# Seven waits for stores behind the block's closing barrier, and no GpSimd drain in that barrier

## Chip, core and metric

The kernel runs on one core of a Trainium2 chip. The metric is the device time of one execution in microseconds (us). Three runs of the kernel before the change took 148.33, 148.35 and 148.73 us; the median is 148.35.

## What is computed

The input x has 2048 rows of 640 numbers (bf16). Each row is normalised, and three things are added: x itself, a spectral filter of the normalised rows, and a two-layer network of them.

```python
def _A_ref(x, w_r, w_i):
    X = rfft2(x.astype(float32), axes=(-2, -1))
    X = X * (w_r + 1j * w_i)
    return irfft2(X, s=(S, D), axes=(-2, -1)).astype(bfloat16)

def _B_ref(x, w1, b1, w2, b2):
    h = gelu(x @ w1 + b1)          # 640 -> 1536
    return h @ w2 + b2             # 1536 -> 640

xn = layernorm(A_x)
out = A_x + _A_ref(xn, A_w_r, A_w_i) + _B_ref(xn, B_w1, B_b1, B_w2, B_b2)
```

## The kernel before

The 2048 rows are worked on as 16 chunks c of 128 rows. Early stages load x and the weights (SyncE's queue, L375), normalise, transpose, run the first layer of the network (results in `gT`) and the forward and inverse transforms as matmuls against tables. TensorE works on all of this nearly without a gap. The last stage, for each chunk c, adds up in PSUM the second layer and the last step of the inverse transform (L383); VectorE adds the bias row and writes the finished chunk into SBUF (L787); one DMA brings it to the output in HBM.

There are 18 such final stores. Chunks 0 to 13 go by GpSimd's queue (L794), each as an accumulating DMA onto a copy of x that was put into the output earlier. Chunks 14 and 15 go by SyncE's queue (L791) as plain DMAs: chunk 14 in one store, chunk 15 in three (320, 160 and 160 columns), since its sum is made in three pieces. So GpSimd issues 14 stores, and SyncE issues 4. Each store has a semaphore of its own, which reaches 16 when the data has landed.

What each engine does, and in which order, is a list written out by hand (`ORDER`, set up by `arrange`). `sync` works out which waits an operation needs, and `emit` puts the lists into the program: it opens a block (`nc.Block()`), in which every engine gets its own body. In a body each operation is preceded by its waits (L233). SyncE's body ends with a loop over the list `last`, that is the 18 stores, and waits for each (L244).

When the block closes, every engine leaves its body by a branch and meets the others at a barrier. The block is closed by the `with ExitStack()` statement, so the profile shows the instructions of that barrier under L319: a DRAIN on each engine, which on four of them counts up a semaphore; GpSimd waits for the four (EVENT_SEMAPHORE) and releases them with a second instruction; each of the four waits for that release. The program opens with a barrier of the same make, which the profile shows under L813. The kernel has no instruction of its own behind the closing barrier.

Of the kernel before, what the change touches and what calls it, by code (L numbers as in the profile page):

```python
# [121 lines left out]
class Sched:  # L122
# [7 lines left out]
    def op(self, engs, prio, emit, reads=(), writes=(), after=(), gate=(), segs=None, dma=None, late=0.0, group=None, hard=()):  # L130
        o = Op()
        o.name = writes[0].name if writes else ""
        o.engs, o.prio, o.emit, o.segs, o.dma, o.late, o.group = engs, prio, emit, segs, dma, late, group
        o.reads, o.writes, o.gate, o.hard = list(reads), list(writes), list(gate), list(hard)
        o.seq = len(self.ops)
        o.eng, o.inc, o.count, o.sem = None, False, None, None
        o.deps = [w for b in o.reads for w in b.writers] + list(after)
        for b in o.reads:
            b.readers.append(o)
        for b in o.writes:  # L140
            b.writers.append(o)
        self.ops.append(o)
        return o
# [69 lines left out]
    def emit(self, es, last):  # L213
        nc = self.nc
        sems = {e: nc.alloc_semaphore(f"s_{e}") for e in self.engines if e != "sp"}
        shared = {g: nc.alloc_semaphore(f"g_{g}") for g in self.groups}
        for e in self.engines:
            n = 0
            for o in self.order[e]:
                if o.group:  # L220
                    o.sem, o.count = shared[o.group], 16 * len(self.groups[o.group])
                elif o.dma:
                    o.sem, o.count = nc.alloc_semaphore(f"d_{o.seq}"), 16
                elif o.inc:
                    n += 1
                    o.sem, o.count = sems[e], n
        block = es.enter_context(nc.Block())

        def run(name):
            def go(e):  # L230
                for o in self.order[name]:
                    for d in o.waits:
                        e.wait_ge(d.sem, d.count)  # L233
                    ins = o.emit(e, name)
                    if o.dma:
                        ins.then_inc(o.sem, 16)
                    elif o.inc:
                        ins.then_inc(o.sem, 1)
                if name == "sp":
                    seen = set()  # L240
                    for o in last:
                        if (o.group or o) not in seen:
                            seen.add(o.group or o)
                            e.wait_ge(o.sem, o.count)  # L244
            return go
        block.sync(run("sp"))
        block.gpsimd(run("pool"))
        block.vector(run("dve"))
        block.scalar(run("act"))
        block.tensor(run("pe"))  # L250
# [46 lines left out]
def bass_parallel_sum__spectral_gfnet__dense_activation_gelu__prompt_kernel(  # L297
# [21 lines left out]
    with ExitStack() as es:  # L319
# [478 lines left out]
        K.sync()  # L798
        K.emit(es, last)


# [1 line left out]
_INS = ['A_x', 'A_w_r', 'A_w_i', 'B_x', 'B_w1', 'B_b1', 'B_w2', 'B_b2']  # L803
# [24 lines left out]
```

## Time and profile before

| what | value |
|---|---|
| median of three runs | 148.35 us |
| the profiled execution, its own time | 148.24 us |
| its span, first to last instruction | 146.4 us |
| granted TensorE clock over the span | 1.000 |
| TensorE matmuls busy | 142.3 us |
| VectorE, ScalarE, GpSimd busy | 110.6, 76.2, 21.4 us |

Times in the profile count from the first instruction of the span. PE is TensorE, DVE VectorE, ACT ScalarE, POOL GpSimd and SP SyncE; a name with a q (SPq, POOLq) is an engine's sequencer, which handles waits, branches and the issue of DMAs. In the rows of one source line, the three numbers behind the count are the shortest, median and longest duration in ns, and "first and last start" are in us. "DMA to landing" counts from the start of the issue to the landing of the data. The execution's own time is longer than its span: something at the start or the end of an execution lies outside the recorded instructions.

### The profile page before, as it was taken

How to read it: one execution, taken by the hardware profiler on the slowest of the kernel's cores; microseconds unless marked ns; L12 is line 12 of the kernel's file. 1: busy time of each engine (PE TensorE's matmuls, PEld its weight loads, DVE VectorE, ACT ScalarE, POOL GpSimd, SP SyncE). 2: the span in 40 equal slices, each digit the busy share in tenths (PEclk: the TensorE clock that was granted, in tenths of full speed). 3: DMA queues.
4: the chain of work that ended last, by engine and by line, in shares of the span. 5: the costliest groups of instructions: out<-in, count | busy, mean ns of one | idle time of the engine just before them, and what ended most of it. 6: DMA issues, size and time to landing. Idle time of an engine off the chain costs nothing.

```text
span 146.4 us, 3965 instructions
## 1 busy us (share of the span) xinstructions
PE 142.3 (97%) x1685; PEld 89.3 (61%) x1685; DVE 110.6 (76%) x237; ACT 76.2 (52%) x125; POOL 21.4 (15%) x35
## 2 busy tenths in 40 slices
PE   7899999999999999999999999999999999999992
PEld 7799995655566545445545455555576665655571
DVE  1898999999994459659959999471059995996571
ACT  3517995158786697887678554143445471300000
POOL 1102031211010041000000000000000125526240
PEclk9999999999999999999999999999999999999999
DMA  4999999669999989908300932515300307976685
GB/s 118 322 396 399 348 385 217 161 135 95 183 176 185 206 230 330 358 23 115 67 4 10 118 63 42 117 24 111 69 4 0 45 5 89 118 81 83 81 100 124
DMA packets 27923, 21.00 MB, mean 143 GB/s; under 512 B 20226, under 2 KB 25090, under 8 KB 27779
## 3 DMA queue, kind: packets, MB, share of 16 engines
q1 hardware_dynamic: 24528, 15.03, 43.5%
q0 software_dynamic: 2592, 4.92, 18.3%
q10 hardware_dynamic: 786, 0.82, 2.4%
q8 instruction: 13, 0.21, 0.6%
q14 instruction: 4, 0.02, 0.0%
HBM read 13.54 MB, written 5.24 MB: 128 GB/s over the span
## 4 chain that ended last, share of the span: by engine, by line
PE 94%; DVE 2%; DMA 2%; issue 0%
PE ps L383 93%; DMA X<-in_A_x_dram 2%; DVE stats L483 1%; PE ps L531 1%; DVE T L513 0%; DVE mv L485 0%; DVE W L787 0%; DVE xnT L395 0%; DVE rstd L491 0%; DVE ve L493 0%
## 5 line engine op out<-in xcount | busy, mean ns | idle before, releaser
L383 PE MATMUL ps<-xnT,W 128*128 128x512 bf16 (+2 forms) x336 | 57.7, 320 | 0.1
L383 PE MATMUL ps<-W,gT 128*128 128x512 bf16 (+3 forms) x396 | 57.6, 296 | 0.0
L383 PEld LDWEIGHTS ps<-W,gT 128*128 128x128 bf16 x396 | 30.1, 98 | 22.8 <-issue 1.5
L383 PEld LDWEIGHTS ps<-xnT,W 128*128 128x128 bf16 x336 | 31.6, 114 | 17.3 <-issue 2.2
L614 ACT ACTIVATE gT<-ps,b1col 128x512 bf16<-128x512 f32 (+1 forms) x48 | 28.9, 637 | 6.8 <-PE ps L383 6.6
L794 POOL DMA_DIRECT2D out_dram<-W x14 | 12.2, 902 | 74.0 <-DVE W L787 74.0
L483 DVE BATCH_NORM_STATS2 stats<-X 128x6 f32<-128x320 bf16 x32 | 13.9, 479 | 2.2 <-DMA X<-in_A_x_dram 2.2
L394 ACT ACTIVATE Wf<-ps 128x960 bf16<-128x960 f32 (+1 forms) x9 | 7.6, 880 | 12.0 <-PE ps L383 7.0
L394 ACT ACTIVATE XV<-ps 128x1280 bf16<-128x1280 f32 (+2 forms) x8 | 8.8, 1104 | 7.7 <-PE ps L383 7.7
L681 DVE TENSOR_TENSOR T<-Y,Wf 128x1288 bf16<-128x1288 bf16 x16 | 12.5, 824 | 0.1
L494 POOL TENSOR_TENSOR rstd<-ve,mhalf 128x2 f32<-128x2 f32 (+1 forms) x8 | 6.2, 770 | 33.1 <-DVE ve L493 33.1
L394 ACT ACTIVATE Xb<-ps 128x960 bf16<-128x960 f32 (+1 forms) x7 | 8.0, 1165 | 3.8 <-PE ps L383 3.8
L395 DVE CAST Y<-ps 128x644 bf16<-128x644 f32 x8 | 6.6, 828 | 4.0 <-PE ps L383 3.9
L547 DVE TENSOR_TENSOR T<-T 128x128 bf16<-128x128 bf16 (+1 forms) x32 | 8.5, 320 | 0.1
L394 ACT ACTIVATE T<-ps 128x512 bf16<-128x512 f32 (+1 forms) x14 | 5.4, 442 | 6.0 <-PE ps L383 6.0
L395 DVE CAST Xb<-ps 128x960 bf16<-128x960 f32 (+1 forms) x5 | 5.5, 1110 | 3.8 <-PE ps L383 3.8
L787 DVE TENSOR_TENSOR W<-ps,X 128x640 bf16<-128x640 f32 x7 | 5.7, 822 | 2.4 <-PE ps L383 2.4
L543 DVE TENSOR_TENSOR T<-T 128x640 bf16<-128x640 bf16 x16 | 7.4, 488 | 0.2
L513 DVE TENSOR_SCALAR T<-X,mv,rstd 128x640 bf16<-128x640 bf16 x16 | 6.7, 432 | 1.1 <-POOL rstd L494 1.1
L394 ACT ACTIVATE Y<-ps 128x644 bf16<-128x644 f32 x8 | 5.7, 708 | 3.4 <-PE ps L383 3.4
L383 PE MATMUL ps<-etab,XV 32*128 32x160 bf16 (+1 forms) x128 | 7.2, 232 | 0.0
L383 PE MATMUL ps<-Wf,htab 128*128 128x512 bf16 (+3 forms) x33 | 7.1, 295 | 0.0
(55 smaller groups left out, 127.4 us busy)
## 6 DMA issues: line engine op xcount, KB each, us to landing
out_dram<-in_A_x_dram POOLq DMA_DIRECT2D x4, 640.0 KB, 7.3
X<-in_A_x_dram SPq DMA_DIRECT2D x7, 320.0 KB, 8.8
out_dram<-W POOLq DMA_DIRECT2D x14, 160.0 KB, 3.5
W<-in_B_w_dram SPq DMA_DIRECT2D x5, 384.0 KB, 5.4
W<-in_B_w_dram SPq DMA_DIRECT2D x3, 640.0 KB, 12.4
Wf<-in_A_w_i_dram SPq DMA_DIRECT2D x7, 160.5 KB, 4.0
Wf<-in_A_w_r_dram SPq DMA_DIRECT2D x5, 160.5 KB, 3.5
gtab<-c_G SPq DMA_DIRECT2D x1, 512.0 KB, 7.4
```

The lines of the kernel that those rows point to most:

```text
L383: ins = e.matmul(o_, lhsT=lw, rhs=rh, start=st, stop=sp_, skip_group_check=True)
L394: return e.activation(dst(), src(), ACT.Copy, scale=scale)
L395: return e.tensor_copy(dst(), src())
L483: st_ops.append(K.op([("dve", 0.393)], pr, lambda e, _, c=c, h=h: e.bn_stats(stats[:, c, 6 * h:6 * h + 6], view(X, c * D + H2 * h, [[1, H2 ...
L494: K.op([("pool", 0.75)], 400 + pr, lambda e, _, a=a, b=b: e.tensor_tensor(out=rstd[:, a:b], in0=ve[:, a:b], in1=mhalf[:, a:b], op=ALU.pow) ...
L513: o = K.op([("dve", 0.356)], pr, lambda e, _, c=c, n=n, xnv=xnv: e.tensor_scalar(out=xnv(n, 0, [[1, D]]), in0=view(X, c * D, [[1, D]]), sc ...
L543: K.op([("dve", 0.39)], pr, lambda e, _, k=k, op=op, xnv=xnv, x1v=x1v: e.tensor_tensor(out=x1v(H2 * k, [[D, 2], [1, H2]]), in0=xnv(0, 0, [ ...
L547: ring_ops.append(K.op([("dve", 0.333 if w == 128 else 0.136)], pr, lambda e, _, op=op, x1v=x1v, xfv=xfv, o_=o_, o0=o0, o1=o1, w=w: e.tens ...
L614: K.op([("act", act_us(128 * nt, 1) + 0.02)], pr + PRIO["gelu"], lambda e, _, c0=c0, nt=nt, fc=fc, hps=hps: e.activation(gT[:, fc, 128 * c ...
L681: filt_ops.append(K.op([("dve", 0.738)], pr, lambda e, _, k=k, Y=Y, TB=TB, pair=pair: e.tensor_tensor(out=view(TT, TB.slot * 8 * KP + k * ...
L787: K.op([("dve", dve_us(w))], 95, lambda e, _, os_=os_, fps=fps, o0=o0, w=w, xo=xo, base=base: e.tensor_tensor(out=view(W1, OST + os_.slot ...
L794: last.append(K.op([("pool", 0.9)], 450, lambda e, _, c=c, os_=os_: e.dma_start(ov[:, c, :], view(W1, OST + os_.slot * D, [[1, D]]), accum ...
```

## The change

SyncE's body no longer ends with waits. The list `rest` holds seven stores: the last three of GpSimd's and all four of SyncE's. SyncE waits for these seven after the block has closed, so behind the barrier. For the other eleven stores of GpSimd, SyncE waits inside its body, ahead of its second store. The block is opened with `no_gpsimd_drain=True`, so that it closes without GpSimd's DRAIN.

```diff
-        block = es.enter_context(nc.Block())
+        stores = {e: [o for o in self.order[e] if o in last] for e in ("pool", "sp")}
+        self.rest = stores["pool"][-3:] + stores["sp"]
+        block = es.enter_context(nc.Block(no_gpsimd_drain=True))
 
         def run(name):
             def go(e):
                 for o in self.order[name]:
+                    if o is stores["sp"][1]:
+                        for d in stores["pool"][:-3]:
+                            e.wait_ge(d.sem, d.count)
                     for d in o.waits:
                         e.wait_ge(d.sem, d.count)
                     ins = o.emit(e, name)
...
                         ins.then_inc(o.sem, 1)
-                if name == "sp":
-                    seen = set()
-                    for o in last:
-                        if (o.group or o) not in seen:
-                            seen.add(o.group or o)
-                            e.wait_ge(o.sem, o.count)
             return go
...
         K.sync()
         K.emit(es, last)
 
+    for o in K.rest:
+        nc.sync.wait_ge(o.sem, o.count)
```

## The prediction

> **What bounds the kernel now.** I read the page first, then the chain that ended last, then the last 2.5 us instruction by instruction, because the change touches nothing earlier.
>
> ```profile
> span 146.4 us, 3965 instructions
> ...
> PE 142.3 (97%) x1685; PEld 89.3 (61%) x1685; DVE 110.6 (76%) x237; ACT 76.2 (52%) x125; POOL 21.4 (15%) x35
> ...
> PE 94%; DVE 2%; DMA 2%; issue 0%
> ```
>
> TensorE sets the time up to its last matmul. What follows is the tail, and the chain of waits in order of time shows where it begins:
>
> ```profile
> 139.80 3.85 PE ps L383 x41
> 143.65 0.03 issue
> 143.68 0.33 DVE W L787
> ```
>
> The last VectorE add ends at 143.68 + 0.33 = 144.01. The span ends at 146.44, so 2.43 us hang on no engine's arithmetic. The table by stretches divides them (columns: the stretch, its length, busy time of PE, PEld, DVE, ACT and POOL, clock, DMA share, GB/s):
>
> ```profile
> 144.00:144.50 0.50, 0.00 (x0) 0.00 (x0) 0.00 (x1) 0.00 (x0) 0.00 (x0) 1.00 0.93 253
> 144.50:145.60 1.10, 0.00 (x0) 0.00 (x0) 0.00 (x0) 0.00 (x0) 0.00 (x0) 1.00 0.22 51
> 145.60:146.44 0.84, 0.00 (x0) 0.00 (x0) 0.00 (x0) 0.00 (x0) 0.00 (x0) 1.00 0.00 0
> ```
>
> In the last 0.84 us no engine computes and no DMA moves a byte. To see what stands there, I took the rows of the last SyncE store, of the waits at L244 (all nine, the first four, the last) and of the closing barrier at L319:
>
> ```profile
> L791 SPq DMA_DIRECT2D out_dram<-W x1: 333/333/333, 144.0 to 144.0; - x1
> ...
> DMA to landing us min/median/max: 1.5/1.5/1.5
> ```
>
> ```profile
> L244 SPq EVENT_SEMAPHORE  x9: 17/28/28, 144.4 to 145.6; - x9
> ...
> L244 SPq EVENT_SEMAPHORE  x4: 17/28/28, 144.4 to 144.6; - x4
> ...
> L244 SPq EVENT_SEMAPHORE  x1: 27/27/27, 145.6 to 145.6; - x1
> ```
>
> ```profile
> L319 POOLq EVENT_SEMAPHORE  x2: 17/17/17, 146.3 to 146.3; - x2
> ...
> L319 POOLq DRAIN  x1: 4570/4570/4570, 140.9 to 140.9; - x1
> L319 PEldq DRAIN  x1: 1435/1435/1435, 142.3 to 142.3; - x1
> L319 DVEq DRAIN  x1: 364/364/364, 143.7 to 143.7; - x1
> L319 SPq COMPARE_BRANCH  x1: 38/38/38, 146.0 to 146.0; - x1
> L319 SPq DRAIN  x1: 13/13/13, 146.2 to 146.2; - x1
> L319 SPq EVENT_SEMAPHORE  x1: 17/17/17, 146.4 to 146.4; - x1
> ...
> L319 PEldq EVENT_SEMAPHORE  x1: 51/51/51, 146.4 to 146.4; - x1
> ```
>
> Read as one line of events: the last store is issued at 144.0 and lands 1.5 later, at 145.5; SyncE's last wait passes at 145.6; its branch comes at 146.0, its DRAIN at 146.2, GpSimd's two barrier instructions at 146.3, the releases at 146.4. So **landing first, then branch, then barrier, one after the other**. TensorE's and VectorE's DRAINs are over by 142.3 + 1.4 = 143.7 and 143.7 + 0.36 = 144.1, GpSimd's by 140.9 + 4.57 = 145.5: in the barrier everybody waits for SyncE, and SyncE comes late because it waited for the landing first.
>
> **The change part by part.** *Moving the seven waits.* SyncE is free after the issue of its fourth store, at 144.0 + 0.33, so by 144.4. With no wait left in its body it goes to the branch and the barrier at once. From the last wait (145.6) to the DRAIN (146.2) the branch cost 0.6 before; a branch without a wait shows in no row here. Bounds: nothing, as on VectorE, whose DRAIN starts at 143.7, with its last add at 143.68; and the same 0.6. From the DRAIN to the end of the releases is 146.44 − 146.2 = 0.2. SyncE is thus through the barrier at 144.4 + (0 to 0.6) + 0.2, between 144.6 and 145.2. I need no choice between the two: both lie before the landing at 145.5, which is the cover of this whole part. The cover has 0.3 us to spare at the worst end.
>
> Behind the barrier stand the seven waits. Before, 18 waits took nine EVENT_SEMAPHOREs and the branch, so about two to an instruction; four that had nothing left to wait for started within 0.2, that is 0.07 each. Seven waits are four instructions (seven if they are not paired): 0.3 to 0.5 if all had to run after the landing, nothing but the last one if they run while the landing is awaited. SyncE arrives at 144.6 to 145.2, and the landings are spread up to 145.5, so the last wait passes when it passes now: 145.6. **What is late next is the landing itself**, and the change does not touch it. Nothing is queued behind the seven waits on SyncE but the end of the program.
>
> *Leaving out GpSimd's DRAIN.* It ran from 140.9 to 145.5. Its last store and the three that `rest` holds:
>
> ```profile
> L794 POOL DMA_DIRECT2D out_dram<-W x1: 862/862/862, 141.0 to 141.0; - x1
> ...
> DMA to landing us min/median/max: 3.8/3.8/3.8
> ```
>
> The store was issued by 141.0 + 0.86 = 141.8 and landed at 140.96 + 3.8 = 144.8; the DRAIN ended 0.7 after that. If it stayed, the barrier could not open before 145.5, then 0.1 for GpSimd's part (146.3 to 146.4) and four to seven waits of 0.07 behind it: 145.5 + 0.1 + (0.3 to 0.5) = 145.9 to 146.1. So this part carries 0.3 to 0.5 of the gain, and it frees GpSimd at 141.8. By the Trainium skill, VectorE: DVE Perf Modes, section "The DRAIN you can't avoid", a boilerplate DRAIN takes a constant 12 ns or so on all five engines. By that rule this part would be worth nothing, and the moved waits alone would give the sum. SyncE's 13 ns agree with it, GpSimd's 4570 ns do not, and the row decides.
>
> *The eleven waits ahead of SyncE's second store.* These are for GpSimd's stores 1 to 11:
>
> ```profile
> L794 POOL DMA_DIRECT2D out_dram<-W x11: 856/862/1216, 113.2 to 134.2; - x11
> ...
> DMA to landing us min/median/max: 3.3/3.5/4.2
> ```
>
> ```profile
> L791 SPq DMA_DIRECT2D out_dram<-W x1: 332/332/332, 141.5 to 141.5; - x1
> ```
>
> ```profile
> 142.68 1.69 SPq L791 DMA_DIRECT2D out_dram<-W  x3
> ```
>
> ```profile
> L791 SPq DMA_DIRECT2D out_dram<-W x1: 396/396/396, 143.1 to 143.1; - x1
> ...
> DMA to landing us min/median/max: 2.1/2.1/2.1
> ```
>
> The eleventh landed by 134.2 + 4.2 = 138.4, so none of them waits. They cost about six instructions of 0.07 = 0.4 and stand between the end of the first store's issue (141.5 + 0.33 = 141.8) and the second's start (142.68): a gap of 0.8 that covers them. Queued behind them are stores 2, 3 and 4. Without the cover, the second store would slip by 0.4 and the third from 143.1 to 143.5; it would land at 143.5 + 2.1 = 145.6 at the latest, level with the fourth. The fourth needs VectorE's last add (144.01) and would not move. So the end could lose 0.1 at most; I take 0.
>
> *The sum.* Span: 146.44 − 0.84 = 145.6, against the profiled execution. That execution took 148.24, so 148.24 − 146.44 = 1.80 lie outside the span, and no row shows what is in them. If they stay, the time is 145.6 + 1.80 = 147.40. They could shrink: four engines are released at 144.6 to 145.2 and no longer together with SyncE, so they may do 0.4 to 1.0 of whatever follows while SyncE still waits. The only rows of such skew are those of the opening barrier:
>
> ```profile
> L813 SPq DRAIN  x1: 7/7/7, 0.0 to 0.0; - x1
> ...
> L813 POOLq DRAIN  x1: 186/186/186, 0.3 to 0.3; - x1
> ...
> L813 SPq EVENT_SEMAPHORE  x1: 17/17/17, 0.7 to 0.7; - x1
> ```
>
> There the engines come up to 0.3 apart. I allow 0 to 0.3 for the shrinking and take 0.1, near the lower end, since nothing shows it: 147.30. The median of the runs shown is 148.35 − 148.24 = 0.11 above the profiled execution, so the forecast for the median is **147.4**, a gain of 0.95 (0.6%).
>
> **The rivals.** *The part outside the span shrinks by more.* The four engines are ahead of SyncE by 0.4 to 1.0. If they use 0.3 to 0.4 of that, the time is 147.5 − 0.35 = 147.15. For it: GpSimd, the slowest at the opening barrier, would be free first. Against it: no row shows any work there. The Trainium skill, Runtime: NRT & Kernel Launch, section "The ~15µs preamble/postamble breakdown", says that a barrier of all engines follows the kernel and takes about 1.5 us; no run here shows it. By that page only SyncE's leg of it would be left, which is this rival.
>
> *The DRAIN stays in effect*, so that the change does not do what it says: the flag leaves a DRAIN in, or something else in the barrier holds GpSimd until 145.5. Then SyncE is through at 145.9 to 146.1, a gain of about 0.5 without any shrinking: 147.85. Against it: nothing but the drain held GpSimd after 141.8.
>
> *The drain comes back outside the span.* What GpSimd did for 0.7 after its last landing is done later, behind SyncE's last wait. The span loses 0.84 and the rest gains 0.7: 148.2. Against it: GpSimd would be free from 141.8, and could do this while SyncE waits.
>
> *Slower: SyncE's own DRAIN waits for its stores.* Before, it ran after all of them had landed, so its 13 ns say nothing of a DRAIN with stores in flight. GpSimd's ended 0.7 after the landing. If SyncE's does so, it ends at 145.5 + 0.7 = 146.2, the same moment as before; the release comes at 146.4, and the seven waits, now behind it, add 0.3 to 0.5: 148.35 + 0.4 = 148.75. It is slower from the point where SyncE's DRAIN ends later than 145.9. Against it: SyncE's issues are 0.33 long and end long before the landing, and GpSimd's DRAIN covers work that GpSimd does itself, in issues of 0.86.
>
> **How the numbers follow.** Forecast 147.4: 0.62. Larger shrinking, 147.15: 0.20. DRAIN stays, 147.85: 0.06. Drain comes back outside, 148.2: 0.06. SyncE's DRAIN waits, 148.75: 0.06. A change within 0.3% (0.45 us, so 147.9 to 148.8) is about what a measurement of this kernel cannot tell from none. Faster by more than that: the first three, 0.88. Within it: the fourth and most of the fifth, 0.09. Slower: 0.03. The range is 147.0 to 147.85: the low end is the larger shrinking with a little scatter of the runs, the high end the forecast with no shrinking (147.5), the 0.1 of the eleven waits and 0.25 of scatter, which takes in the DRAIN that stays; the last two cases, 0.12, are left out.
>
> **What would show it.** In the profile of the changed kernel: no DRAIN of POOL in the closing barrier; SyncE's DRAIN between 144.4 and 145.0 and releases by 145.2; the last store issued at 144.0 as before and landed 1.5 later; the span closed by SyncE's last EVENT_SEMAPHORE at about 145.6; the second SyncE store still at 142.7. I am wrong if SyncE's DRAIN starts or ends after 145.5, if GpSimd's barrier instructions come that late, if the last store lands later than 145.6, or if the span falls by 0.84 and the time does not.

## The result, and the profile after

The changed kernel takes 147.14 us (median of six runs, 146.71 to 149.69), the kernel before 148.34 (six runs). The ratio is 0.9915, 95% interval 0.989 to 0.994, so 0.6 to 1.1% faster; the forecast was 147.4. One of the six runs, the one of 149.69, was disturbed (its clock was 0.988) and is left out of the ratio. The profiled execution took 147.20, with a span of 145.91.

The last VectorE add and the last SyncE store in the kernel after:

```profile
144.01 0.33 DVE W L786
```

```profile
L790 SPq DMA_DIRECT2D out_dram<-W x1: 332/332/332, 144.4 to 144.4; - x1
...
DMA to landing us min/median/max: 1.5/1.5/1.5
```

The last add starts 0.33 later than in the profile before (143.68). That lies ahead of the tail, in a part which the change does not touch; this start moved from 143.56 to 144.81 over the ten profiles of this study. I therefore measure the tail from the start of the last add to the end of the span. Before it was 146.44 − 143.68 = 2.76, after it is 145.91 − 144.01 = 1.90: **0.86 less**. The closing barrier (L318 here) and the four instructions that hold the seven waits (L801), in the profile after:

```profile
L318 SPq EVENT_SEMAPHORE  x2: 17/17/17, 144.9 to 145.1; - x2
L318 POOLq EVENT_SEMAPHORE  x2: 17/17/17, 145.0 to 145.1; - x2
L318 SPq DRAIN  x1: 143/143/143, 144.7 to 144.7; - x1
...
L318 PEldq EVENT_SEMAPHORE  x1: 51/51/51, 145.1 to 145.1; - x1
```

```profile
L801 SPq EVENT_SEMAPHORE  x4: 17/28/28, 145.6 to 145.9; - x4
```

SyncE's DRAIN starts as soon as the store is issued (144.36 + 0.33 = 144.7), the releases come at 145.1, and the last wait passes at 145.9, when the store has landed (144.36 + 1.5). GpSimd has no DRAIN in this barrier any more. Landing and barrier, one behind the other before, now run beside each other. The landing itself has not moved: it comes 1.86 us after the start of the last add before (145.54) and 1.85 after (145.87).

Two things are not as foretold. Between the release of SyncE at 145.1 and its first wait behind the barrier at 145.6 there is nearly half a us in which nothing shows, though the store which that wait is for (the first of SyncE's) had landed at about 145.15. And outside the span there are 147.20 − 145.91 = 1.29 us, not 1.80. The second adds to the gain: 0.86 + 0.51 = 1.37, less the 0.33 of the late start, is the 1.04 by which the two profiled executions differ.

For all kernels below, each line gives the median time, the ratio to the kernel before, the tail of the one profile, and the range, over the runs that the ratio counts, of what lies outside the span (time less span, the span to 0.1):

| kernel | median us | ratio, 95% interval | tail | outside |
|---|---|---|---|---|
| before | 148.28 to 148.34 | 1 | 2.76 | 1.74 to 1.86 |
| after | 147.14 | 0.9915, 0.989 to 0.994 | 1.90 | 1.24 to 1.31 |
| after, again | 146.94 | 0.9895, 0.985 to 0.994 | 1.90 | 1.28 to 1.31 |
| waits moved, DRAIN kept | 147.93 | 0.9983, 0.996 to 1.000 | 2.74 | 1.26 to 1.37 |
| no DRAIN, waits as before | 148.32 | 1.0006, 0.999 to 1.003 | 2.83 | 1.74 to 1.83 |
| before, ten more waits | 147.85 | 0.9961, 0.994 to 0.998 | 2.34 | 1.75 to 1.87 |
| eight early waits on ScalarE | 147.34 | 0.9947, 0.992 to 0.997 | 1.90 | 1.79 to 1.88 |
| the same, SyncE padded | 146.94 | 0.9901, 0.987 to 0.994 | 1.93 | 1.29 to 1.34 |
| all 18 waits behind | 147.21 | 0.9929, 0.990 to 0.996 | 2.23 | 1.28 to 1.37 |
| seven waits on ScalarE | 147.20 | 0.9919, 0.989 to 0.995 | 1.91 | 1.42 to 1.50 |

Tail and outside together say more than the medians, because they leave out what varies ahead of the tail.

### The profile page after: what moved, and what is told of

It is laid out like the page before. It is cut to its first block, busy times and chain, and to the rows that moved or that the text cites. A ratio compares the mean times of both kernels' runs of the same rounds, so it can differ in the third digit from the quotient of the medians.

```text
span 145.9 us, 3953 instructions
## 1 busy us (share of the span) xinstructions
PE 141.5 (97%) x1670; PEld 89.6 (61%) x1685; DVE 110.6 (76%) x237; ACT 76.3 (52%) x125; POOL 21.4 (15%) x35
## 4 chain that ended last, share of the span: by engine, by line
PE 93%; DMA 3%; issue 1%; SPq 1%; DVE 0%
PE ps L382 92%; DMA W<-in_B_w_dram 3%; SPq L374 1%; PE ps L530 1%; DVE W L786 0%
## 5 line engine op out<-in xcount | busy, mean ns | idle before, releaser
L382 PE MATMUL ps<-W,gT 128*128 128x128 bf16 (+3 forms) x381 | 55.3, 292 | 1.4 <-issue 1.0
```

Source lines behind the costliest of these rows:

```text
L382: ins = e.matmul(o_, lhsT=lw, rhs=rh, start=st, stop=sp_, skip_group_check=True)
```

## The experiments

The theory after the result: the end of the kernel is one chain of landing, barrier, one late SyncE instruction, and something that all engines do after the span. The change lays the barrier, the late instruction and the other engines' share of that something beside the landing. The rivals are named at each run.

**The waits moved, the DRAIN kept.**

```diff
-        block = es.enter_context(nc.Block(no_gpsimd_drain=True))
+        block = es.enter_context(nc.Block())
```

> The waits are moved as in the change; GpSimd's DRAIN stays. Theory (the end of the kernel is one chain: landing, SyncE's late 80th instruction, barrier, what follows; the drain is long enough to hold the barrier): the DRAIN ends 0.7 us after GpSimd's last landing, that is at about 145.7, the releases come at 145.8, then SyncE loses 0.47 before its first wait behind the barrier and is done at 146.5 to 146.6; with 1.3 outside the span about 147.9, so 0.4 to 0.5 below before. Rival (the gain is the moved waits alone, a drain is a formality): as the changed kernel, 147.1.

It took 147.93. In its profile the last add, the barrier and the waits:

```profile
143.85 0.33 DVE W L786
```

```profile
L318 POOLq EVENT_SEMAPHORE  x2: 17/17/17, 145.7 to 145.8; - x2
...
L318 POOLq DRAIN  x1: 4570/4570/4570, 141.1 to 141.1; - x1
...
L318 SPq DRAIN  x1: 143/143/143, 144.6 to 144.6; - x1
```

```profile
L801 SPq EVENT_SEMAPHORE  x4: 17/28/28, 145.9 to 146.6; - x4
...
L801 SPq EVENT_SEMAPHORE  x3: 28/28/28, 146.4 to 146.6; - x3
```

SyncE is at the barrier at 144.7, and GpSimd's DRAIN holds everybody until 141.11 + 4.57 = 145.7. Only then come SyncE's waits: the first at 145.9, the second not before 146.4, all for stores that had landed by 145.7. The tail is as long as before (2.74 against 2.76). The whole gain of this kernel, some 0.4 by the medians, lies outside the span (1.3), with the DRAIN in place. As a time it is not clear of noise (the interval of the ratio reaches 1.000); what lies outside the span is.

**No DRAIN, the waits as before.**

```diff
-        block = es.enter_context(nc.Block())
+        block = es.enter_context(nc.Block(no_gpsimd_drain=True))
```

> GpSimd's DRAIN is left out; all 18 waits stay in SyncE's body. Theory: SyncE comes last to the barrier anyway, so the time is that of before, 148.3 (0.05 more or less), with 1.8 us outside the span. Rival (what shrank outside the span from 1.8 to 1.3 in the changed kernel is the missing drain, not the early release of the four other engines): 1.3 outside the span, 147.85.

It took 148.32, ratio 1.0006, with 1.74 to 1.83 outside. So the DRAIN's absence is worth nothing by itself, and it is not what shrank the part outside the span. (The tail of 2.83 is 0.07 longer: without GpSimd's DRAIN the profile has one instruction more on SyncE in the barrier, a DRAIN and then a signal, where before the DRAIN counted up the semaphore itself.) What this run and the one before have apart is when the four other engines are released: at 145.8 to 145.9 with SyncE done at 146.6 there, and together with SyncE here.

**The kernel before with ten settled waits on SyncE.** In SyncE's body of the kernel before, ahead of its first final store:

```diff
                 for o in self.order[name]:
+                    if name == "sp" and o is [p for p in self.order["sp"] if p in last][0]:
+                        for d in [p for p in self.order["sp"] if p.dma and not p.group and p not in last][:10]:
+                            e.wait_ge(d.sem, d.count)
```

This asks what the gap of 0.47 before SyncE's branch was. Counted in the trace, the branch was SyncE's 80th recorded instruction in the kernel before, and the first wait behind the barrier is its 80th in the kernel after; in both the 80th starts 0.47 after the one ahead of it, without a wait that explains it.

> The kernel before with ten more waits on SyncE, for loads that landed long ago, ahead of its first final store: five more instructions, at a place where SyncE has 38 us of nothing to do. Theory (in both kernels it is SyncE's 80th recorded instruction that comes 0.47 us late, whatever it is): the late instruction is now one of the waits at the end, which await landings anyway; the branch follows the last wait within 0.1 and the time falls by 0.4 to 0.47 to 147.9. Rival (the 0.47 belongs to a branch, or to a branch that carries a wait): the branch comes 0.47 after the last wait as before, 148.35 to 148.4.

It took 147.85. The waits at the end (L247 here) up to 145.1 and from there on, and the barrier:

```profile
L247 SPq EVENT_SEMAPHORE  x4: 17/28/28, 144.8 to 145.0; - x4
...
L247 SPq EVENT_SEMAPHORE  x6: 28/28/28, 145.0 to 145.9; - x6
```

```profile
L322 SPq COMPARE_BRANCH  x1: 41/41/41, 146.0 to 146.0; - x1
L322 SPq DRAIN  x1: 7/7/7, 146.2 to 146.2; - x1
```

The branch now follows the last wait at once (145.9, then 146.0), and the tail is 2.34, 0.42 shorter, with more instructions than before. The late one is again the 80th: the fifth wait, 0.47 after the fourth (which ends at 145.0 and stands in both rows), at a place where SyncE has to await landings anyway. The 0.47 thus belongs to a place in SyncE's sequence of instructions and not to the branch.

**Eight early waits on ScalarE.** The changed kernel, with SyncE four instructions shorter:

```diff
-                        for d in stores["pool"][:-3]:
+                        for d in stores["pool"][8:-3]:
...
+                if name == "act":
+                    for d in stores["pool"][:8]:
+                        e.wait_ge(d.sem, d.count)
```

> The changed kernel, with eight of SyncE's eleven early waits given to ScalarE, which has been idle since 128 us: SyncE has four instructions fewer, 79 recorded instead of 83. Theory (the 80th instruction comes late): no instruction of the kernel comes late any more and the four waits behind the barrier follow the release at once, but the first one that follows the kernel on SyncE does, behind the last landing, so the part outside the span grows from 1.3 to about 1.75 and the time is 147.55. Rival (the 0.47 belongs to the first wait behind a barrier, or to the branch): it stays where it was, hidden under the landing, and the time is 147.1.

It took 147.34, between the two forecasts as a median, but what lies outside the span settles it: 1.79 to 1.88 in nine runs, against 1.24 to 1.31 for the changed kernel. Within the span nothing is late any more:

```profile
L321 SPq EVENT_SEMAPHORE  x1: 17/17/17, 144.6 to 144.6; - x1
```

```profile
L804 SPq EVENT_SEMAPHORE  x4: 17/28/28, 144.8 to 145.4; - x4
```

The release is at 144.6 and the first wait at 144.8, where the kernel after has 145.1 and 145.6. SyncE has 79 recorded instructions, and the time outside grew by some 0.5. That SyncE's next instruction, the first behind the kernel, is the late one has no row of its own here.

**The same, SyncE padded.** To part SyncE's count from ScalarE's new waits, eight settled waits (four instructions) ahead of SyncE's first final store:

```diff
+                    if o is stores["sp"][0]:
+                        for d in [p for p in self.order["sp"] if p.dma and not p.group and p not in last][:8]:
+                            e.wait_ge(d.sem, d.count)
```

> The kernel with eight early waits on ScalarE, and eight waits for loads that landed long ago put on SyncE ahead of its first final store, so that SyncE has its 83 recorded instructions again. Theory (the 80th instruction of SyncE comes late): the late one is again the first behind the barrier, hidden under the landing; outside the span 1.3 us instead of 1.83, and 147.1. Rival (the 0.53 outside the span came from ScalarE's eight waits, not from SyncE's count): 1.83 outside, 147.35 to 147.6.

It took 146.94, as the changed kernel itself in the same session (146.94), with 1.29 to 1.34 outside. ScalarE's waits cost nothing that shows; SyncE's count was the cause.

**All 18 waits behind the barrier.** The waits ahead of the second store go, and `rest` holds all stores:

```diff
-        self.rest = stores["pool"][-3:] + stores["sp"]
+        self.rest = stores["pool"] + stores["sp"]
...
-                    if o is stores["sp"][1]:
-                        for d in stores["pool"][:-3]:
-                            e.wait_ge(d.sem, d.count)
```

> The changed kernel with all 18 waits behind the barrier, so without those ahead of SyncE's second store. Theory: SyncE is through the barrier 0.4 before the last landing is due, as in the changed kernel; nine instructions of 0.07 and the late 80th stand behind it, 0.6 + 0.47 = 1.1 in all, against the 0.75 that there are until the last landing; so SyncE is done 0.3 later than in the changed kernel: 147.4. Rival (settled waits cost nothing behind the barrier): 147.1.

It took 147.21, 0.27 more than the changed kernel beside it. The intervals of the two ratios overlap, so the profile has to carry it:

```profile
143.64 0.33 DVE W L783
```

```profile
L798 SPq EVENT_SEMAPHORE  x6: 27/28/28, 144.8 to 145.2; - x6
...
L798 SPq EVENT_SEMAPHORE  x3: 27/28/28, 145.7 to 145.9; - x3
```

Six instructions run in 0.4, the 80th comes late at 145.7, and the last starts at 145.85. The last store was issued 0.03 after its add had ended, as in the changed kernel, and so had landed some 0.35 earlier. The tail is 2.23 against 1.90. The nine waits and the late instruction no longer fit under the landing together. The waits alone would have fitted, by an estimate: nine of 0.07 from 144.8 on end at 145.4, and the landing came at 145.5.

**The seven waits on ScalarE.**

```diff
     for o in K.rest:
-        nc.sync.wait_ge(o.sem, o.count)
+        nc.scalar.wait_ge(o.sem, o.count)
```

> The changed kernel with the seven waits behind the barrier on ScalarE instead of SyncE. Theory (the engines that do not wait do their part of what follows early; what is left is that of the waiting one): the span ends with ScalarE's last wait, where SyncE's ended; the part outside the span stays near 1.3 if the two engines' part that is left is equally long, and is up to 0.5 longer if ScalarE has to be there earlier than SyncE: 147.1 to 147.6, and I take 147.25. Rival (what follows is short because SyncE is the one that waits, being free otherwise): 1.8 outside, 147.6.

It took 147.20 with 1.42 to 1.50 outside, 0.1 to 0.2 more than with SyncE as the waiting engine; the tail is the same (1.91).

```profile
L801 ACTq EVENT_SEMAPHORE  x4: 17/38/38, 145.1 to 145.7; - x4
```

Most of the 0.5 stays won whichever of the two engines waits, so it comes from the early release of the others. SyncE is the better one by 0.1 to 0.2 outside the span; as times the two kernels are not told apart (their intervals overlap). Here SyncE has only 79 recorded instructions, but it is free from 144.9: an instruction that came 0.47 later would start at 145.4, while ScalarE waits until 145.7, and the part outside does not show it.

**The changed kernel once more**, beside the last three:

> The changed kernel once more, beside the three below on the same chip. Both theories: 147.1, with 1.3 outside the span.

It took 146.94, with 1.28 to 1.31 outside.

## Why the prediction was right, and where it was off

*Landing, branch and barrier stand one behind the other, and moving the waits lays them side by side.* Right. The tail fell by 0.86; the forecast was 0.84. SyncE was to be through the barrier between 0.6 and 1.2 after the start of the last store's issue; it was through 0.75 after it (145.1 against 144.36), and the last wait passed with the landing. One sign of being wrong came up, a last store that lands later than 145.6 (145.87), but with the late start of the last add; from that start on the landing took as long as before.

*"From the last wait (145.6) to the DRAIN (146.2) the branch cost 0.6."* The bound held, the name was wrong. In the kernel after the DRAIN follows the last issue by 0.04 and no branch shows. The barrier took more than the 0.2 of the sum: 0.38 from the start of SyncE's DRAIN (144.74) to the end of its release (145.12), so that SyncE's time came out inside the bounds with one term at nothing and the next too small. What cost 0.47 was the 80th instruction, and it did not vanish: it turned up behind the barrier (145.1 to 145.6). There it is covered, but closely: the four waits had 0.07 to spare before the landing, where I had counted 0.3.

What makes the 80th late stays open, but an instruction fetch goes with this place. In nine of the ten profiles the last packet that the DMA view lists under "instruction" (queue q14, 8 KB) starts 1.08 to 1.11 us after the end of SyncE's 79th instruction, and 1.31 after it in the kernel before. The release of the barrier keeps no such distance: it lies anywhere from 1.9 ahead of that packet to 0.2 behind it. In the kernel with ten more waits the packet comes at 146.10, still inside the span, and it is the only one of any queue from 145.95 on (packets, MB, and the share of that stretch):

```profile
q14 instruction: 1, 0.01, 9.0%
```

In the two kernels whose SyncE ends with its 79th, the packet lies behind the span (146.55 and 146.01). So the packet keeps to this place of SyncE's list even where the kernel has no 80th. The 80th starts 0.6 us or more ahead of the packet, so it does not wait for that one. The Trainium skill, Runtime: NRT & Kernel Launch, section "Instruction fetch mechanics", says that a sequencer gets its instructions in blocks and that crossing from one to the next is mostly hidden. A boundary between the 79th and the 80th would fit the fixed place and the packet, but where the 80th stood in the kernel before, its 0.47 was not hidden, and no run shows that such a boundary is what takes the 0.47.

*The DRAIN carries 0.3 to 0.5 of the gain.* Right in kind, too small. With the DRAIN kept the tail is 2.74, so leaving it out is worth 0.84 once the waits are moved: behind the held barrier the late 80th instruction has nothing to cover it either, and 0.84 less its 0.47 is 0.37, inside the range foretold. By itself it is worth nothing (1.0006), since SyncE was last anyway. The two parts of the change need each other: each alone gave at most 0.5 (2.76 + 1.80 less 2.74 + 1.33 for the moved waits, the profiled execution of which took 147.92 with a span of 146.59), both together 1.2 to 1.4. The Trainium skill's 12 ns for a boilerplate DRAIN (VectorE: DVE Perf Modes, "The DRAIN you can't avoid") had to be put aside here as well: 4570 ns on GpSimd in the run that kept it, and 143 on SyncE with stores in flight. But the Trainium skill says it there of the DRAINs in the runtime's preamble and postamble; the one at issue closes the kernel's own block, so the rule need not cover it.

*The eleven waits are hidden.* Right, but for 0.07:

```profile
L236 SPq EVENT_SEMAPHORE  x5: 17/28/28, 142.2 to 142.5; - x5
```

```profile
143.08 1.62 SPq L790 DMA_DIRECT2D out_dram<-W  x3
```

Five of their instructions are over at 142.5. The last two waits stand beside the store's own wait for its add (a sixth instruction at 143.01, and the issue itself), and the second store goes out at 143.08, 0.10 after that add has ended and not 0.02 as before. The third store follows its add as closely as before, so the end loses nothing. With all 18 waits behind the barrier the tail was longer by 0.33.

*The part outside the span: 0.1 taken of 0 to 0.3.* This term was mis-sized: it shrank by 0.5. It is the reason that the result lies 0.26 under the forecast. By this term alone it would lie 0.4 under it; the rest is less than the runs of one kernel differ by (146.71 to 147.54), and the second set of runs (146.94) lies 0.46 under. So the rival that the part shrinks by more had the right side, and that its 147.15 meets 147.14 almost exactly is luck, since it allowed 0.3 to 0.4. I had the mechanism, four engines that go ahead while SyncE waits, and took a value near the lower end because no row shows that stretch. But it could be read: it is the time less the span, and it is 1.74 to 1.87 whenever all engines are released together and 1.24 to 1.37 when the other four are released 0.7 or more before SyncE is done (unless SyncE's 80th instruction falls behind its last wait). That a barrier of all engines follows, as the Trainium skill says (Runtime: NRT & Kernel Launch, "The ~15µs preamble/postamble breakdown"), agrees with this. The stretch itself has no rows of instructions, so its steps are not shown, nor that only SyncE's leg of such a barrier is left, as the prediction worked it out.

*The other rivals.* The DRAIN did not stay in effect. It did not come back outside the span: 1.3 there with and without it. SyncE's DRAIN did not wait for the stores: 143 ns, and about 1 us before the last landing.

## What to carry to other kernels

At the end of a kernel, first write down what stands behind the last landing; whatever of it does not need the landing can be laid beside it by waiting behind the barrier, provided nothing else holds the barrier. Test the two halves of such a change apart: here the missing DRAIN alone shows nothing and the moved waits alone some third of what both give (by the tail and what lies outside the span). And subtract the span from the time in every run: a constant that jumps from 1.8 to 1.3 is a term of the sum, even though no row shows it.

## What the runs showed of the hardware

SyncE's 80th recorded instruction started 0.47 us after the end of the one ahead of it in every profile where it lies in the kernel (the kernels before and after, and five of the others), be it a branch or a wait. Five settled instructions put where SyncE was idle moved that delay under a wait, and the kernel before became 0.44 us faster by the medians (0.9961); four instructions taken away pushed it behind the end, and what lies outside the span grew by 0.5. A packet on the instruction queue starts 1.08 to 1.11 us after the instruction ahead of that place has ended (1.31 in the kernel before). GpSimd's DRAIN ended 0.8 us after its last store had landed and took 4.5 to 4.6 us in all three profiles that have it. Settled waits of SyncE ran at 0.07 us each, two semaphores to an instruction.
